# Twenty matmuls over a tile of ones in the first block of tokens, and other planning costs for early attention

## The chip, the cores and the metric

The kernel runs on one NeuronCore of a Trainium2 chip. The metric is the device time of one launch in microseconds (us). The engines are TensorE (PE in the profile, with its weight loads shown apart as PEld), VectorE (DVE), ScalarE (ACT), GpSimd (POOL), and SyncE (SP), whose queue issues nearly all the DMAs.

## What is computed

The reference is a chain of three layers on 2304 tokens of width 512. In short:

```python
scores = q @ k.T / 8 + slope[h] * -(distance)      # 4 x 8 heads, 576 tokens, width 64
scores = where(0 <= i - j < 128, scores, -1e9)     # a window of 128
x = softmax(scores) @ v                            # to 2304 x 512
h = x @ w_in                                       # 512 -> 2048
x = (h - tanh(h)) @ w_out                          # 2048 -> 512
xn, en = x / norm(x), expert_emb / norm(expert_emb)
logits = xn @ en.T / tau                           # 8 experts, the best one is taken
out = gate * (relu(x[mask] @ w1[e]) @ w2[e])       # 512 -> 1024 -> 512 for each expert
```

## The kernel before

The 2304 tokens are 18 blocks of 128, worked on two at a time (9 groups). A block's attention is cut into four quarters of two heads. A quarter is a chain over the engines: scores on TensorE (`scores`, L456, into the PSUM tile `sc`), bias and row minimum on VectorE (`soft`, L484), exponent on ScalarE (`exp`, L498), a turn of the probabilities on TensorE (`tr_pe`, L518), its copy to SBUF on ScalarE or VectorE (`tr_out`, L524, tile `ptf`), and the product with v on TensorE (`pv_f`, L535, tile `of`). This form, called early, holds for the first four blocks and runs on plain fp32 tiles; later blocks split their operands into high and low parts and turn the probabilities by DMA. A finished block is turned by four transposes (L633) into `xT`, and the two-layer part follows in steps: `g1` (L686, tile `h`, 12 matmuls of 256 columns each), tanh and a split on ScalarE and VectorE (L691 to L703), `g2` (L710, tile `acc`).

The 32 weight tiles of w_in and w_out come from HBM as 64-bit floats, each 512 KB (`rawi`, `rawo`). Each is converted by hand: a first reading on ScalarE (L325), two long integer operations on VectorE (L328, L331), and some scaling, rounding and subtracting on ScalarE, VectorE or GpSimd (L307 to L317). Nothing of a step can start before the four weight tiles that it uses are through this.

The order of the instructions on each engine is fixed when the program is built. `Plan.add` takes a task with a cost in us for each engine that could do it, a due number, and what it reads and writes; `Plan.order` places tasks one by one, each time the one that can start first by these costs (the due number decides between equals), and the engines then run their lists strictly in that order, with semaphores between them. A cost in the plan thus sets only the order and the choice of engine, never how long something takes.

At the start, `small` fills a few constants on GpSimd, among them `ones`, a 128x128 tile of bf16 ones (L237), which is first read much later, for counting tokens per expert.

Of the kernel before, what the change touches and what calls it, by code (L numbers as in the profile page):

```python
# [10 lines left out]
F32 = mybir.dt.float32  # L11
# [38 lines left out]
AHEAD = 1.5  # L50
WRATE = 1.0
WRATE2 = 1.0
PAD = 8
FA = 4
PADN = 2
# [107 lines left out]
class Builder:  # L163
# [55 lines left out]
    def consts(self, P):  # L219
# [8 lines left out]
        for h in range(H):  # L228
# [3 lines left out]
        P.add({"POOL": 0.5}, lambda e: nc.gpsimd.tensor_copy(out=self.tri, in_=at[0][:, 256:384]), -11,  # L232
              r=[("xr", 0)], w=["tri"])

    def small(self):
        nc, i = self.nc, self.i
        nc.gpsimd.memset(self.ones, 1.0)  # L237
        nc.gpsimd.memset(self.half, 0.5)
        nc.gpsimd.memset(self.cum, 0.0)
        nc.gpsimd.memset(self.oh, 0.0)  # L240
        for j in range(self.NOV):
            nc.gpsimd.memset(self.thr[:, :, j:j + 1], float(128 * j))
# [193 lines left out]
    def quarter(self, P, a, due):  # L436

        nc = self.nc
        b, qd = divmod(a, 4)
        hf, qq = divmod(qd, 2)  # L440
        s, n = b % 2, (2 * b + hf) % 2
        one = b in NOPRE
        W = 128 if one else 256
        v = {"sc": [None, None], "mx": [None, None]}
        pb = a % 2 if a < NPX else 0
# [4 lines left out]
        def scores(jj):  # L450
            sc = v["sc"][jj] = self.scores[jj][:, 0]
            j = qq + 2 * jj
            hp, p0 = hf * 4 + j, 64 * jj
            if early:
                x = slice(1, 2) if one else slice(0, 2)
                nc.tensor.matmul(sc[:, 0:W // 128, :], lhsT=self.qf[b // 2][p0:p0 + 64, b % 2, hf * 2 + qq, :],  # L456
                                 rhs=self.kf[max(b, 1)][p0:p0 + 64, x, hf * 2 + qq, :], start=True, stop=True)
                return
            q = self.qst[n]
            sl = s if one else slice(0, 2)  # L460
            for m in range(2):
                nc.tensor.matmul(sc[:, sl, :], lhsT=q[:, m, j, :], rhs=self.khl[:, sl, hp, :], start=(m == 0),  # L462
                                 stop=(m == 1))
# [116 lines left out]
        ttr += 0.13 * (2 * (b in SPLIT) + (b - 1 in SPLIT))  # L580
        for jj in range(2):
            if early:
                P.add({"PE": 0.45 if one else 0.65}, lambda e, jj=jj: scores(jj), due,
                      r=["at", ("qf", b)] + [("kf", max(b, 1), x) for x in ([1] if one else [0, 1])], w=[("sc", jj)])
            else:
                P.add({"PE": 0.11 if one else 0.22}, lambda e, jj=jj: scores(jj), due,
                      r=["at"] + ks + [("kl", x, hf) for x in kv] + q, w=[("sc", jj)])
# [7 lines left out]
        half = [("xr", 2 * hf), ("xr", 2 * hf + 1)]  # L595
        if early:
            for jj in range(2):
                P.add({"PE": 0.28 if one else 0.5}, lambda e, jj=jj: tr_pe(jj), due, r=["at", "con", ("p32", pb, jj)],
                      w=[("tp", jj)])
            for jj in range(2):  # L600
                P.add({"ACT": 0.3, "DVE": 0.29} if one else {"ACT": 0.38, "DVE": 0.42}, lambda e, jj=jj: tr_out(e, jj),
                      due, r=["at", ("tp", jj)], w=[("pt", a % 2, 1)] if jj else [("pt", a % 2), ("pt", a % 2, 1)])
            P.add({"PE": 0.85 if one else 1.65}, pv_f, due,
                  r=["at", ("pt", a % 2), ("pt", a % 2, 1)] + [("vf", x) for x in ([b] if one else [b - 1, b])], w=[("o", qq)] if qq else ["o", ("o", 0), ("o", 1)])
            if qq:
                P.add({"DVE": 0.5}, recip, due, r=["at"], w=sm)
                P.add({"DVE": 0.4}, mul, due, r=["at", "o", ("o", 0), ("o", 1)] + sm, w=half if hf else [("xr", m) for m in range(4)])
            return
# [557 lines left out]
    def build(self):  # L1166
# [7 lines left out]
        self.px = dp.tile([2 * N0, 128, DM], F32, name="px")  # L1174
        self.pa = dp.tile([2 * N0, 128, DM], F32, name="pa")
        P = Plan()
        P.add({"POOL": 0.6}, lambda e: self.small(), 0, w=["small", "cum"])
        self.consts(P)
        self.small_loads(P, -9)
        self.emb(P, -9)  # L1180
# [237 lines left out]
```

## Time and profile before

| what | us |
|---|---|
| median of three runs (843.29 to 847.38) | 847.1 |
| the profiled execution, whole | 849.56 |
| its span, from first to last instruction | 847.8 |
| TensorE busy in the span | 816.7 (96%) |
| VectorE busy | 565.5 (67%) |
| ScalarE busy | 441.6 (52%) |
| GpSimd busy | 252.1 (30%) |

The profiled execution lies 2.5 us above the median. The profile splits the span into stretches that differ in what they do: the first 66 us hold the early attention and the first steps, then the weight conversion runs on to about 143 us, and the rest is the steady run of steps, later attention, routing and experts. The shares of the whole span say little about the first two.

### The profile page before, as it was taken

What the parts mean: (1) busy time and instruction counts of PE and PEld (TensorE: products, weight loads), DVE (VectorE), ACT (ScalarE), POOL (GpSimd) and SP (SyncE); (2) the same over time, 40 slices, a digit from 0 to 9 for tenths busy, and PEclk for the clock granted to TensorE, in tenths of its full rate; (3) what the DMA queues carried; (4) which work ended last, traced back from release to release, by engine and by line L of the source; (5) the groups of instructions that cost most, each with busy time, mean ns of one, the idle gap of its engine ahead of it and who ended that gap; (6) DMA issues with size and microseconds to landing.
All of it is one profiled execution on the core that took longest, in us unless ns stands there. A gap on an engine that the chain in (4) does not pass through costs nothing.

```text
span 847.8 us, 15246 instructions
## 1 busy us (share of the span) xinstructions
PE 816.7 (96%) x5244; PEld 721.2 (85%) x5244; DVE 565.5 (67%) x1500; ACT 441.6 (52%) x997; POOL 252.1 (30%) x246
## 2 busy tenths in 40 slices
PE   6999999999999999999999999999999999999995
PEld 4677878988888899988998998989889899998994
DVE  4658999987778577777776775576366656666230
ACT  3759876665555355555554543464255545545120
POOL 1424676554424233324242240021110210111011
PEclk9999999999999999999999999999999999999998
DMA  8973325945334234433434312365266656555000
GB/s 299 334 268 121 109 94 160 270 107 130 96 82 135 40 82 106 87 87 91 99 83 102 80 41 48 125 212 162 84 198 216 216 166 189 193 163 174 20 27 30
DMA packets 109464, 112.88 MB, mean 133 GB/s; under 512 B 62901, under 2 KB 75189, under 8 KB 109248
## 3 DMA queue, kind: packets, MB, share of 16 engines
q1 hardware_dynamic: 106240, 102.35, 42.2%
q0 software_dynamic: 3136, 9.46, 3.0%
q8 instruction: 43, 0.70, 0.4%
q14 instruction: 45, 0.37, 0.1%
HBM read 87.12 MB, written 17.48 MB: 123 GB/s over the span
## 4 chain that ended last, share of the span: by engine, by line
PE 71%; DVE 11%; DMA 7%; issue 6%; ACT 2%; SPq 2%; POOL 1%; POOLq 0%; DVEq 0%; ACTq 0%
PE h L686 19%; PE acc L710 17%; PE he L1014 9%; PE y L1049 8%; PE o L546 3%; DMA pt<-ph 3%; PE sc L456 3%; PE sc L462 2%; DMA out<-yo,ix 2%; DVE wst L331 2%; PE y L1045 2%; PE misc L785 2%; PE of L535 2%; DVE rawo L328 1%; PE sc L518 1%
## 5 line engine op out<-in xcount | busy, mean ns | idle before, releaser
L686 PE MATMUL h<-xT,wi 128*128 128x256 f32 x1728 | 228.8, 287 | 0.0
L686 PEld LDWEIGHTS h<-xT,wi 128*128 128x128 f32 x1728 | 219.4, 193 | 6.4 <-issue 2.6
L710 PE MATMUL acc<-wo,gh 128*128 128x512 f32 x576 | 183.9, 400 | 0.0
L710 PE MATMUL acc<-wo,gl 128*128 128x512 f32 x288 | 112.9, 392 | 2.0 <-DVE gl L703 2.0
L710 PEld LDWEIGHTS acc<-wo,gh 128*128 128x128 f32 x576 | 99.7, 189 | 15.1 <-issue 0.7
L691 ACT ACTIVATE t<-h 128x512 f32<-128x512 f32 x72 | 43.1, 599 | 100.3 <-PE h L686 95.3
L1049 PE MATMUL y<-eo,ge 128*128 128x512 f32 x336 | 88.5, 399 | 0.0
L484 DVE CUSTOM_DVE_ANT_0 sc<-sc,bias 128x256 f32<-128x256 f32 (+1 forms) x144 | 52.7, 372 | 46.3 <-PE sc L462 29.4
L498 ACT ACTIVATE p<-sc,mx 128x256 f32<-128x256 f32 (+1 forms) x128 | 59.3, 464 | 34.1 <-DVE mx L484 26.0
L1074 POOL DMA_INDIRECT out<-yo,ix x24 | 23.4, 975 | 176.2 <-PE y L1045 61.0
L1049 PEld LDWEIGHTS y<-eo,ge 128*128 128x128 f32 x336 | 60.0, 188 | 9.7
L710 PEld LDWEIGHTS acc<-wo,gl 128*128 128x128 f32 x288 | 54.1, 188 | 15.1 <-DVE gl L703 2.9
L508 POOL TENSOR_TENSOR ph<-p,ph 128x512 f16<-128x512 f32 (+1 forms) x38 | 46.1, 1214 | 69.3 <-ACT ph L503 26.0
L703 DVE TENSOR_TENSOR gl<-t,gh 128x512 fp32r<-128x512 f32 x72 | 63.0, 876 | 4.6 <-ACT gh L699 4.4
L948 DVE TENSOR_TENSOR eo<-est,eo 128x512 fp32r<-128x512 f32 x60 | 45.0, 752 | 30.4 <-ACT eo L944 29.4
L1036 DVE SCALAR_TENSOR_TENSOR ge<-he,ge 128x256 fp32r<-128x256 f32 x104 | 29.9, 325 | 51.9 <-ACT ge L1030 51.9
L694 DVE TENSOR_TENSOR t<-h,t 128x512 f32<-128x512 f32 x72 | 49.5, 687 | 19.0 <-ACT t L691 19.0
L944 ACT CAST eo<-est 128x512 fp32r<-128x512 f32 x64 | 39.7, 620 | 40.1 <-PE y L1045 21.5
L1014 PE MATMUL he<-xT,ei 128*128 128x320 f32 x384 | 60.4, 309 | 0.0
L1014 PEld LDWEIGHTS he<-xT,ei 128*128 128x128 f32 x384 | 58.3, 188 | 2.3
L1030 ACT ACTIVATE ge<-he 128x320 fp32r<-128x320 f32 (+1 forms) x56 | 24.1, 430 | 67.5 <-PE he L1014 61.7
L1014 PE MATMUL he<-xA,ei 128*128 128x320 f32 (+1 forms) x384 | 59.0, 302 | 0.0
(181 smaller groups left out, 1425.6 us busy)
## 6 DMA issues: line engine op xcount, KB each, us to landing
est<-in_w SPq DMA_DIRECT2D x128, 256.0 KB, 2.9
rawi<-in_w_in SPq DMA_DIRECT2D x16, 512.0 KB, 6.6
rawo<-in_w_out SPq DMA_DIRECT2D x16, 512.0 KB, 7.3
stk<-in_k SPq DMA_DIRECT2D x30, 256.0 KB, 2.7
stq<-in_q SPq DMA_DIRECT2D x28, 256.0 KB, 2.8
bucket<-in_c_pad SPq DMA_DIRECT2D x8, 771.0 KB, 5.8
xe<-bucket SPq DMA_DIRECT2D x17, 257.0 KB, 3.5
vst<-in_v SPq DMA_DIRECT2D x30, 128.0 KB, 2.4
```

The source lines that it names most:

```text
L484: nc.vector.tensor_tensor_reduce(out=x, in0=x, in1=self.bias[:, h, c0:c1], scale=-0.125, scalar=mx[:, 1:2] if m else 3.0e38, op0=ALU.add, ...
L498: nc.scalar.activation(out=v["p32"][:, jj * W:(jj + 1) * W], in_=x, func=AF.Exp, scale=-1.0, bias=v["mx"][jj][:, 0:1], accum_out=self.sums ...
L508: self.eng(e).tensor_tensor(out=ph[:, 2 * W:4 * W], in0=v["p32"][:, 0:2 * W], in1=ph[:, 0:2 * W], op=ALU.subtract)
L686: nc.tensor.matmul(h3(v["h"], f2), lhsT=w[:, a, k, :], rhs=xT[c][:, :, k, :], start=(k == 0 and n == 0), stop=(k == KD - 1 and n == 2))
L691: nc.scalar.activation(out=v["t"], in_=v["h"].rearrange("p a b -> p (a b)"), func=AF.Tanh)
L694: nc.vector.tensor_tensor(out=v["t"], in0=v["h"].rearrange("p a b -> p (a b)"), in1=v["t"], op=ALU.subtract)
L703: self.eng(e).tensor_tensor(out=v["gl"], in0=v["t"], in1=v["gh"].bitcast(F32), op=ALU.subtract)
L710: nc.tensor.matmul(self.acc[g, t], lhsT=v[a][:, c0:c0 + 128], rhs=self.w["o", fs[f2]][:, c, :], start=(first and f2 == 0 and n == 0), stop ...
L944: nc.scalar.copy(out=t[:, 0, :], in_=v["x"])
L948: self.eng(eng).tensor_tensor(out=t[:, 1, :], in0=v["x"], in1=t[:, 0, :].bitcast(F32), op=ALU.subtract)
L1014: nc.tensor.matmul(h[:, 0:N], lhsT=w[:, a, c0:c0 + 128], rhs=xT()[b][:, k, 0:N], start=(k == 0 and n == 0), stop=(k == KD - 1 and n == 2))
L1049: nc.tensor.matmul(y[t], lhsT=gt(f, a)[:, (t - ts[0]) * 128:(t - ts[0] + 1) * 128], rhs=self.w["o", f0 + f][:, b, :], start=(f == 0 and n ...
```

## The change

The fill of `ones` is taken out of `small` and made a task of its own that is due first. A new function `warm` adds 20 tasks to the plan, each one matmul of `ones` with `ones` over 512 columns (bf16) into the PSUM bank `acc0`, which nothing else uses until the first step. Their results are never read. Each has a cost of 0.43 in the plan and due number 0, later than that of the attention tasks, so that the plan puts them where TensorE would have nothing else to start. The planning costs of the three TensorE tasks of early attention are set lower, to about 0.53 to 0.71 of what they were. Data and results are otherwise the same.

```diff
--- before.py
+++ after.py
@@ -50,6 +50,7 @@
 AHEAD = 1.5
 WRATE = 1.0
 WRATE2 = 1.0
+NWARM = 20
 PAD = 8
 FA = 4
 PADN = 2
@@ -232,9 +233,22 @@
         P.add({"POOL": 0.5}, lambda e: nc.gpsimd.tensor_copy(out=self.tri, in_=at[0][:, 256:384]), -11,
               r=[("xr", 0)], w=["tri"])
 
+    def warm(self, P):
+
+        nc = self.nc
+        at = {}
+
+        def mm(e):
+            if 0 not in at:
+                at[0] = self.psA.tile([128, 512], F32, tag="acc0", name="idle", bufs=1)
+            nc.tensor.matmul(at[0], lhsT=self.ones, rhs=self.ones.unsqueeze(1).to_broadcast([128, 4, 128]), start=True,
+                             stop=True)
+
+        for n in range(NWARM):
+            P.add({"PE": 0.43}, mm, 0, r=["ones"])
+
     def small(self):
         nc, i = self.nc, self.i
-        nc.gpsimd.memset(self.ones, 1.0)
         nc.gpsimd.memset(self.half, 0.5)
         nc.gpsimd.memset(self.cum, 0.0)
         nc.gpsimd.memset(self.oh, 0.0)
@@ -580,7 +594,7 @@
         ttr += 0.13 * (2 * (b in SPLIT) + (b - 1 in SPLIT))
         for jj in range(2):
             if early:
-                P.add({"PE": 0.45 if one else 0.65}, lambda e, jj=jj: scores(jj), due,
+                P.add({"PE": 0.3 if one else 0.42}, lambda e, jj=jj: scores(jj), due,
                       r=["at", ("qf", b)] + [("kf", max(b, 1), x) for x in ([1] if one else [0, 1])], w=[("sc", jj)])
             else:
                 P.add({"PE": 0.11 if one else 0.22}, lambda e, jj=jj: scores(jj), due,
@@ -595,12 +609,12 @@
         half = [("xr", 2 * hf), ("xr", 2 * hf + 1)]
         if early:
             for jj in range(2):
-                P.add({"PE": 0.28 if one else 0.5}, lambda e, jj=jj: tr_pe(jj), due, r=["at", "con", ("p32", pb, jj)],
+                P.add({"PE": 0.2 if one else 0.33}, lambda e, jj=jj: tr_pe(jj), due, r=["at", "con", ("p32", pb, jj)],
                       w=[("tp", jj)])
             for jj in range(2):
                 P.add({"ACT": 0.3, "DVE": 0.29} if one else {"ACT": 0.38, "DVE": 0.42}, lambda e, jj=jj: tr_out(e, jj),
                       due, r=["at", ("tp", jj)], w=[("pt", a % 2, 1)] if jj else [("pt", a % 2), ("pt", a % 2, 1)])
-            P.add({"PE": 0.85 if one else 1.65}, pv_f, due,
+            P.add({"PE": 0.45 if one else 0.9}, pv_f, due,
                   r=["at", ("pt", a % 2), ("pt", a % 2, 1)] + [("vf", x) for x in ([b] if one else [b - 1, b])], w=[("o", qq)] if qq else ["o", ("o", 0), ("o", 1)])
             if qq:
                 P.add({"DVE": 0.5}, recip, due, r=["at"], w=sm)
@@ -1174,7 +1188,9 @@
         self.px = dp.tile([2 * N0, 128, DM], F32, name="px")
         self.pa = dp.tile([2 * N0, 128, DM], F32, name="pa")
         P = Plan()
-        P.add({"POOL": 0.6}, lambda e: self.small(), 0, w=["small", "cum"])
+        P.add({"POOL": 0.3}, lambda e: nc.gpsimd.memset(self.ones, 1.0), -30, w=["ones"])
+        self.warm(P)
+        P.add({"POOL": 0.6}, lambda e: self.small(), 0, r=["ones"], w=["small", "cum"])
         self.consts(P)
         self.small_loads(P, -9)
         self.emb(P, -9)
```

On TensorE, the program begins with nine pairs of `LDWEIGHTS ones` and `MATMUL idle` ahead of the first two score matmuls, and four more behind these. The next piece is the start of the list of before, from the first scores (`sc_92` and `sc_93` are the two score tiles, `p` and `p32x` probabilities, `con` the identity matrix):

```order
L456 MATMUL sc_92<-kf_128,qf_126 128x128
L456 MATMUL sc_93<-kf_128,qf_126 128x128
L518 MATMUL sc_92<-con,p_160 128x128
L456 MATMUL sc_92<-kf_128,qf_126 128x128
L269 MATMUL misc<-con,ec 128x8 x4
L518 MATMUL sc_93<-con,p_160 128x128
L456 MATMUL sc_93<-kf_128,qf_126 128x128
L518 MATMUL sc_92<-con,p32x 128x128
L456 MATMUL sc_92<-kf_128,qf_126 128x128
```

The same place now, from the last of the four pairs behind the first scores:

```order
L244 LDWEIGHTS ones
L244 MATMUL idle<-ones 128x512
L532 MATMUL sc_92<-con,p_173 128x128
L470 MATMUL sc_92<-kf_131,qf_128 128x128
L283 MATMUL misc<-con,ec 128x8 x4
L532 MATMUL sc_93<-con,p_173 128x128
L470 MATMUL sc_93<-kf_131,qf_128 128x128
L244 LDWEIGHTS ones
L244 MATMUL idle<-ones 128x512
```

The first turn of probabilities (L518, now L532) stood right behind the first scores and now has 13 of the 20 added matmuls ahead of it, four of them between the two; the other seven follow, in ones and twos, up to the end of the first block. Behind them no added matmul stands.

On VectorE, the list of before at its first weight tile, in the last quarter of the first block (`rawi` and `wst` belong to the weight conversion; `sm`, `sc`, `mx`, `xr` and `ptf` to attention):

```order
L309 TENSOR_SCALAR wst<-rawi_203 128x512
L328 SCALAR_TENSOR_TENSOR rawi_203<-rawi_203 128x512
L553 TENSOR_SCALAR sm<-sm 128x4
L554 RECIPROCAL sm<-sm 128x4
L484 ISA sc_92,mx_260<-sc_92,bias 128x256
L484 ISA mx_260 128x1
L484 ISA sc_93,mx_267<-sc_93,bias 128x256
L484 ISA mx_267 128x1
L331 SCALAR_TENSOR_TENSOR wst<-wst,rawi_203 128x512
L572 TENSOR_TENSOR xr<-of,sm 128x256
L313 CAST wi_283<-wst 128x512
L328 SCALAR_TENSOR_TENSOR rawi_220<-rawi_220 128x512
```

The same place now:

```order
L323 TENSOR_SCALAR wst<-rawi_223 128x512
L538 COPY ptf<-sc_92 128x128
L567 TENSOR_SCALAR sm<-sm 128x4
L568 RECIPROCAL sm<-sm 128x4
L498 ISA sc_92,mx_279<-sc_92,bias 128x256
L498 ISA mx_279 128x1
L498 ISA sc_93,mx_284<-sc_93,bias 128x256
L498 ISA mx_284 128x1
L586 TENSOR_TENSOR xr<-of,sm 128x256
L342 SCALAR_TENSOR_TENSOR rawi_223<-rawi_223 128x512
L538 COPY ptf<-sc_92 128x256
L345 SCALAR_TENSOR_TENSOR wst<-wst,rawi_223 128x512
```

The two long operations of the first weight tile (L328 and L331, now L342 and L345) have moved behind the softmax of the next quarter and the output of the block before; attention is taken a little earlier against the weights. Further down the two lists hold the same tasks in about the same mixture.

## Rows read from the trace of the kernel before

**Rows 1.** The page: busy time of the engines, and the granted clock in 40 slices
```profile
PE 816.7 (96%) x5244; PEld 721.2 (85%) x5244; DVE 565.5 (67%) x1500; ACT 441.6 (52%) x997; POOL 252.1 (30%) x246
...
PEclk9999999999999999999999999999999999999998
```

**Rows 2.** The chain of waits from 5 to 66 us: share by line
```profile
by line: PE sc L456 34.7%; PE of L535 21.5%; PE sc L518 14.6%; PE h L686 14.1%; DMA ec<-in_emb 5.0%; PE misc L633 3.1%; ACT wst L307 1.7%; ACT ptf L524 1.7%; ACT p L498 1.5%; issue 1.5%; ACT p32x L498 1.5%; ACT rawi L325 0.9%; PE misc L269 
```

**Rows 3.** The chain of waits from 66 to 143 us: share by line
```profile
by line: DVE wst L331 23.9%; DVE rawo L328 16.2%; DVE rawi L328 11.1%; DVE gl L703 10.9%; DVE t L694 6.3%; issue 6.0%; DVE sc L484 4.6%; DVE xT L646 3.2%; DVE sm L553 3.1%; DVE wst L309 2.3%; DVE wo L317 2.2%; ACT ptf L524 1.5%; DVE sc L469
```

**Rows 4.** Busy time of each engine by stretch (header names the columns)
```profile
core 0: us, PE busy (x) PEld busy (x) DVE busy (x) ACT busy (x) POOL busy (x), PEclk, DMA share, GB/s
8.00:20.00 12.00, 12.00 (x39) 8.08 (x38) 5.70 (x27) 5.25 (x18) 1.27 (x1) 1.00 1.01 351
20.00:40.00 20.00, 19.00 (x65) 12.93 (x64) 12.25 (x33) 14.66 (x40) 7.73 (x7) 1.00 1.03 357
40.00:66.00 26.00, 26.00 (x96) 19.82 (x94) 16.11 (x40) 15.46 (x40) 6.37 (x7) 1.00 0.73 265
66.00:80.00 14.00, 13.23 (x83) 9.75 (x83) 11.91 (x29) 12.46 (x33) 4.68 (x3) 1.00 0.18 63
80.00:143.00 63.00, 57.54 (x374) 50.49 (x374) 62.10 (x81) 48.84 (x96) 46.99 (x32) 1.00 0.36 114
143.00:848.00 705.00, 687.47 (x4588) 619.15 (x4588) 453.72 (x1278) 342.87 (x767) 182.97 (x173) 0.99 0.43 120
```

**Rows 5.** TensorE in order of time, 54 to 76 us: start, us, what
```profile
54.99 1.80 PE L535 MATMUL of<-vf,ptf 128*128 128x64 f32 x8
...
57.88 2.93 PE L686 MATMUL h<-xT,wi 128*128 128x256 f32 x12
...
61.16 1.22 PE L456 MATMUL sc<-kf,qf 64*128 64x256 f32 x2
62.31 2.93 PE L686 MATMUL h<-xT,wi 128*128 128x256 f32 x12
...
67.51 1.71 PE L686 MATMUL h<-xT,wi 128*128 128x256 f32 x12
69.06 1.00 PE L535 MATMUL of<-vf,ptf 128*128 128x64 f32 x8
...
71.17 0.70 PE L456 MATMUL sc<-kf,qf 64*128 64x256 f32 x2
...
73.01 0.73 PE L710 MATMUL acc<-wo,gh 128*128 128x512 f32 x2
```

**Rows 6.** Who VectorE waited for, 5 to 66 us: total, times, longest
```profile
DVE sc L484 <- ACT ptf L524: 11.2, 11, 2.4
```

**Rows 7.** All engines in order of time, 0 to 9 us
```profile
0.86 0.20 POOL L237 MEMSET ones<- 128x128 bf16 x1 [0.29 <-POOLq L1410]
...
5.46 0.80 PE L456 MATMUL sc<-kf,qf 64*128 64x128 f32 x4 [5.46 <-DMA kf<-in_k]
...
7.30 0.47 PE L518 MATMUL sc<-con,p 128*128 128x128 f32 x1 [1.04 <-ACT p L498]
```

**Rows 8.** Line 325, the first reading of a weight tile, up to 66 us
```profile
L325 ACT ACTIVATE rawi<-rawi x11: 667/678/717, 16.5 to 65.8; 128x512 int32<-128x512 uint32 x11
L325 ACT ACTIVATE rawo<-rawo x6: 645/677/687, 28.7 to 64.7; 128x512 int32<-128x512 uint32 x6
...
  DMA rawi<-in_w_in: 0.4, 1
```

**Rows 9.** DMA issues up to 36 us: count, KB each, us to landing
```profile
rawi<-in_w_in SPq DMA_DIRECT2D x10, 512.0 KB, 8.6
rawo<-in_w_out SPq DMA_DIRECT2D x6, 512.0 KB, 8.5
```

**Rows 10.** TensorE alone: one thin stretch, and after the last matmul
```profile
120.70:124.00 3.30, 1.54 (x7) 1.00 0.90 318
840.00:842.00 2.00, 0.00 (x0) 0.71 0.36 135
```

## Prediction

> **What bounds the kernel now.** I read the page first. TensorE is busy 96% of the span, and the granted clock reads full in all slices but the last [rows 1], so the page alone says that only less TensorE work can help. I then asked which instructions the chain of waits runs over, stretch by stretch, because the share is a mean over stretches with different limits. Up to 66 us the chain is TensorE's: scores 34.7%, product with v 21.5%, turns 14.6%, first steps 14.1% [rows 2]. From 66 to 143 us it is VectorE's, above all the two long operations of the weight conversion [rows 3]; VectorE is then busy 62.10 of the 63 us from 80 on [rows 4]. Behind 143 us TensorE is busy 687.47 of 705 us, and nothing of that stretch is touched.
>
> Next I compared one form with itself at different times, which no share shows. Twelve `h` matmuls took 2.93 us at 62.31 and 1.71 us at 67.51; a pair of scores 1.22 us at 61.16 and 0.70 at 71.17; eight products with v 1.80 at 54.99 and 1.00 at 69.06 [rows 5]. The ratios are 0.58, 0.57 and 0.56, in three forms, all within some 5 us. [...] Before the rise TensorE was busy nearly all the time, but with short fp32 pieces; it rose at the end of the stretch with the `h` matmuls of 62.31. A TensorE that looks busy with such pieces had thus stayed at the low level for 60 us.
>
> **What the change does, part by part.**
>
> *The clock.* Nine matmuls of 512 columns run in a row from about 1.1 us, when `ones` is filled (0.86 + 0.20, [rows 7]), with no operand from HBM; four more follow the first scores. They are dense like the `h` matmuls that came just before the rise. I take it that the clock rises at about 8 us instead of 66. At the low level 12 matmuls of 256 columns take 2.93 us, 0.24 each, so one of 512 columns is at most about 0.49 us there, and at the full level at most 0.73 / 2 = 0.37 (two of `acc`, [rows 5]); both are estimates from a group with its last end in it.
>
> *TensorE's own saving.* From 8 to 66 us it was busy 12.00 + 19.00 + 26.00 = 57.0 us [rows 4]. At 0.575 of that it needs 32.8 us: 24.2 us less. That is the gain if nothing else holds it up.
>
> *What is late next.* In the same 58 us VectorE did 5.70 + 12.25 + 16.11 = 34.1 us of work and ScalarE 5.25 + 14.66 + 15.46 = 35.4 us [rows 4]. This work has to be done as well before the state of 66 us is reached. Much of VectorE's idle time was a wait in attention: 11.2 us ahead of `soft`, put down to ScalarE's copy, which itself lies behind TensorE's turn [rows 6]. How densely VectorE and ScalarE work when TensorE is at full level and the rest is the same mixture of attention and conversion, is shown by the stretch from 66 to 80 us: 11.91 and 12.46 of 14 us, 85% and 89% [rows 4]. At these densities 34.1 us of VectorE take 40.0 us, and 35.4 us of ScalarE 39.7 us. Begun at 8 us, the state of 66 us is reached at 48: 18 us earlier. TensorE's 32.8 us fit in that. This is the term that I take, not the 24.2, since VectorE bounds the next 77 us as well and nothing in them gets faster.
>
> *What comes off.* The first nine added matmuls need up to 9 x 0.49 = 4.4 us, from 1.1 to 5.5 us, and TensorE waited for the first k until 5.46 [rows 7], so they are hidden there, or cost 0.1 us. The next four (up to 2.0 us at the low level) stand ahead of the first turn, which waited 1.04 us for ScalarE [rows 7]: they delay it by up to 0.9 us. The last seven cost at most 7 x 0.37 = 2.6 us at the full level, and lie in the slack that TensorE then has (40 us for 33 us of work). The filling of `ones` moves ahead of nothing that waits. The first weights can't come earlier: the DMA engines' share is 1.01 and 1.03 from 8 to 40 us [rows 4], and ScalarE's first reading of a weight, at 16.5 us, waited for its DMA [rows 8]. By 66 us 17 weights had been read [rows 8]; 16 were issued by 36 us and landed 8.5 us later [rows 9], by about 45, so for a state reached at 48 us they come just in time. I take 1 us for that.
>
> *The planner's costs and the moved tasks.* They shift the conversion of the first tiles on VectorE a little behind attention. VectorE's total is unchanged, and it is the total that I have counted; I set this at nothing, between -2 us (attention, on which TensorE waits, comes earlier) and +2 us (weights come later in the stretch that VectorE bounds).
>
> *The sum.* 18.0 - 0.9 - 1 = 16 us. The profiled execution took 849.56 us, so 833.5; it lies 2.5 us above the median, so the median should be 831 us.
>
> [...]
>
> **The rivals.**
> - *The clock doesn't rise early.* The added matmuls come in a burst, then scores stand between, and attention goes on in short pieces, with which TensorE stayed low for 60 us. The burst is longer than one `h` group (2.93 us); but one group alone, at 57.88 us, was followed by scores that still took 1.22 us, at 61.16 [rows 5], so the rise isn't certain. If the clock rises only with the `h` matmuls again, the added work stands in TensorE's chain: 0.1 + 0.9 + 7 x 0.49 = 4.4 us, and the median is 851.5: slower. Each us that the clock rises later costs some 16 / 58 = 0.28 us of the gain, and 12 us at the full level pay for the last seven matmuls (3.4 us): it decides from a rise later than about 54 us.
> - *It rises and falls back.* Early attention alone may not hold it. For this: nothing in the trace shows a long stretch of attention alone at the full level. Against it: at 120.7 to 124.0 us TensorE was busy 1.54 of 3.30 us and stayed up, and the level fell only after the last matmul, at 840 to 842 us [rows 10]; from 69.06 to 73.01 only attention ran, at the full level [rows 5]. If it is low for half of the 40 us, half the gain is left: 8 us, 839. [...]
> - *The transfers hold it.* If the conversion before 40 us can't move at all, since its weights arrive at the DMA engines' full rate, only the 26 us from 40 to 66 shrink: VectorE's 16.11 us at 85% take 18.9 us, a gain of 7.1 us, 840. Against it: VectorE itself waited mostly for attention there [rows 6].
> - *VectorE gets no gaps at all.* From 8 to 143 us it was busy 34.1 + 11.91 + 62.10 = 108.1 of 135 us [rows 4]; with no idle time left, 26.9 us are gained: 820. For this it would need to be denser than from 66 to 80 us, while ScalarE has its share in every quarter.
>
> **How the numbers follow.** The forecast (824 to 836) has 0.55, the full gain 0.06, the falling back 0.06, the transfers 0.07, no early rise 0.20, and a rise somewhere in between, which leaves 1 to 4 us, 0.06. About half a per cent, 4.2 us, can be told from no change. The first four are faster: 0.74, less 0.02 for their edges. Of no early rise, at 851.5 with the limit at 851.3, I give 0.14 to slower and 0.06 to the same, to which the rise in between adds its 0.06 and the edges 0.02. The range has to reach over no early rise, since it alone holds 0.20: 821 to 852. The forecast's own range is 824 to 836.
>
> **What would show it.** In the changed profile: the `idle` matmuls from about 1.1 us; pairs of scores of 256 columns at 0.70 us, not 1.22, from the second block on; the first `h` group at 1.7 us and some 12 to 18 us earlier than at 50; the chain of waits going over from TensorE to VectorE or ScalarE before 30 us; VectorE's dense stretch ending at about 127 us, not 143; and the stretch behind it as long as before. Pairs of scores at 1.22 us up to 50 us would show the prediction wrong; so would early pairs at 0.70 with the dense stretch still ending at 143.

## The result and the profile after

The changed kernel took 851.1 us (median of 20 runs, 846.38 to 855.65) against 846.2 us of the kernel before in the same sessions (20 runs): a ratio of 1.0067, 95% interval 1.0054 to 1.0080. It is 0.7% slower. The forecast was 831 us and faster: wrong in its sign, though the range 821 to 852 holds the time. That 851.1 lies beside the 851.5 of the rival without an early rise is chance, since the clock did rise early here, at 6.63 us. The profiled execution of the changed kernel took 849.39 us, 0.17 us less than that of before; the two medians lie 4.9 us apart. At 849.56 us the traced execution of before took longer than any of its 20 runs (843.29 to 848.67). So differences between these two traces show where time moves, and the sizes come from the medians and ratios below.

The page after, as in [rows 1]: busy time, and the granted clock in 40 slices of 21.2 us.

```profile
PE 816.5 (96%) x5264; PEld 716.8 (85%) x5264; DVE 570.0 (67%) x1500; ACT 440.5 (52%) x993; POOL 257.5 (30%) x250
...
PEclk9579899999999999999999999999999999999998
```

The clock now has a dent in the second and third slices, and a smaller one in the fifth. TensorE in order of time (start, us, what, and in brackets the idle time before it) answers to [rows 5] and [rows 7]:

```profile
1.12 4.02 PE L244 MATMUL idle<-ones 128*128 128x512 bf16 x9 [1.12 <-POOL half L252]
5.16 0.80 PE L470 MATMUL sc<-kf,qf 64*128 64x128 f32 x4
5.89 1.38 PE L244 MATMUL idle<-ones 128*128 128x512 bf16 x4
7.11 0.27 PE L532 MATMUL sc<-con,p 128*128 128x128 f32 x1
...
19.91 0.70 PE L470 MATMUL sc<-kf,qf 64*128 64x256 f32 x4
20.54 1.28 PE L549 MATMUL of<-vf,ptf 128*128 128x64 f32 x8
23.23 0.44 PE L532 MATMUL sc<-con,p32x 128*128 128x128 f32 x2 [1.41 <-ACT p32x L512]
23.60 1.15 PE L470 MATMUL sc<-kf,qf 64*128 64x256 f32 x2
...
25.30 1.22 PE L470 MATMUL sc<-kf,qf 64*128 64x256 f32 x2
...
46.49 2.93 PE L700 MATMUL h<-xT,wi 128*128 128x256 f32 x12
...
50.92 1.72 PE L700 MATMUL h<-xT,wi 128*128 128x256 f32 x12
```

The burst does what was forecast of it: the record has the clock at full from 6.63 us, the first scores begin at 5.16 us instead of 5.46, and the first turn at 7.11 instead of 7.30. At 19.91 us four score matmuls take 0.70 us. But at 23.60 us two of them take 1.15 us and then 1.22, as before, and this lasts until an `h` group ends at about 51 us: the first group at 46.49 us takes 2.93 us, the next 1.72. The record has the lower level, 0.50 of the full clock, from 23.70 to 51.01 us. So full speed was won from 6.6 to 23.7 us and from 51 to 66 us, and not between.

The stretches after (us, busy time and count of PE, PEld, DVE, ACT, POOL, then granted clock, share of the DMA engines, GB/s):

```profile
8.00:24.00 16.00, 12.82 (x70) 8.14 (x69) 11.30 (x39) 10.30 (x34) 2.16 (x2) 0.99 1.05 367
24.00:51.00 27.00, 27.00 (x87) 17.54 (x86) 15.26 (x40) 14.79 (x40) 9.32 (x8) 0.50 0.97 340
51.00:66.00 15.00, 14.61 (x102) 11.87 (x103) 11.92 (x32) 12.44 (x35) 3.84 (x3) 1.00 0.60 196
66.00:143.00 77.00, 69.40 (x415) 59.55 (x415) 73.04 (x96) 58.08 (x115) 50.33 (x34) 0.96 0.39 129
143.00:200.00 57.00, 54.76 (x417) 49.11 (x416) 48.94 (x153) 35.52 (x93) 36.68 (x36) 1.00 0.66 164
```

The same stretches of the kernel before:

```profile
8.00:24.00 16.00, 15.67 (x50) 10.35 (x50) 8.04 (x34) 8.44 (x27) 2.60 (x2) 1.00 1.00 349
24.00:51.00 27.00, 26.33 (x91) 18.21 (x90) 17.24 (x46) 17.83 (x49) 9.83 (x10) 1.00 0.92 322
51.00:66.00 15.00, 15.00 (x60) 12.27 (x59) 8.78 (x23) 9.09 (x24) 2.94 (x3) 1.00 0.71 264
66.00:143.00 77.00, 70.78 (x456) 60.25 (x456) 74.01 (x109) 61.30 (x128) 51.68 (x35) 1.00 0.33 105
143.00:200.00 57.00, 55.28 (x419) 50.33 (x420) 46.30 (x148) 36.34 (x92) 29.37 (x31) 1.00 0.71 188
```

VectorE is 3.3 us ahead at 24 us, 1.3 us ahead at 51 and 4.4 us ahead at 66. From 24 to 51 us, with both kernels at the low level (pairs of scores at 1.22 us in both), the changed order does *less* of VectorE's work (15.26 us against 17.24). The two lists of VectorE do not go on in about the same mixture, as the section on the change has it: counted in the traces, the second long operation (L331, now L345) of the tenth tile is VectorE's 125th instruction before and its 147th after. TensorE's idle time from 66 to 200 us is 7.60 + 2.24 = 9.8 us, against 6.22 + 1.72 = 7.9 before. The waits of TensorE after, from 66 to 200 us (total us, times, longest):

```profile
PE h L700 <- DVE t L708: 4.2, 3, 3.3
PE sc L476 <- POOL qst L384: 1.3, 1, 1.3
PE o L560 <- DMA pt<-ph: 1.3, 2, 0.8
PE h L700 <- POOL wi L331: 1.2, 3, 0.8
```

The last subtraction of the weight conversion, before on VectorE and after on GpSimd, in order of time:

```profile
140.64 1.77 DVE L317 TENSOR_TENSOR wo<-wst,wo 128x512 fp32r<-128x512 f32 x1
```
```profile
144.79 1.28 POOL L331 TENSOR_TENSOR wo<-wst,wo 128x512 fp32r<-128x512 f32 x1 [1.28 <-ACT wo L327]
```

The conversion was to end at about 127 us; it ends at 146.1 us, 3.7 us later than before. Counted by the ends of groups of 12 `h` matmuls, the changed kernel leads by 6.4 to 7.5 us at the 7th to the 10th group (86 to 102 us) and by 4.7 us at the 25th (149.6 against 154.3), and is 0.5 us behind at the 34th (191.5 against 191.0). The lead is earned before 90 us, and given back between 95 and 191 us, a stretch in which the change has moved the order and added nothing.

### The profile page after: what moved, and what is told of

It reads as the page before. It is cut to its first block, busy times and chain, and to the rows that moved or that the text cites. A ratio compares the mean times of both kernels' runs of the same rounds, so it can differ in the third digit from the quotient of the medians.

```text
span 847.6 us, 15293 instructions
## 1 busy us (share of the span) xinstructions
PE 816.5 (96%) x5264; PEld 716.8 (85%) x5264; DVE 570.0 (67%) x1500; ACT 440.5 (52%) x993; POOL 257.5 (30%) x250
## 4 chain that ended last, share of the span: by engine, by line
PE 69%; DMA 9%; DVE 8%; issue 6%; ACT 3%; SPq 2%; POOL 2%; POOLq 0%; DVEq 0%; ACTq 0%
PE h L700 18%; PE acc L724 15%; PE he L1028 10%; PE y L1063 8%; DMA pt<-ph 5%; PE o L560 3%; DMA out<-yo,ix 2%; PE y L1059 2%; PE sc L470 2%; PE sc L476 2%; DVE wst L345 2%; PE of L549 2%; PE misc L799 1%; PE sc L532 1%; DVE gl L717 1%
## 5 line engine op out<-in xcount | busy, mean ns | idle before, releaser
L700 PEld LDWEIGHTS h<-xT,wi 128*128 128x128 f32 x1728 | 220.2, 194 | 13.2 <-DVE t L708 5.0
L1088 POOL DMA_INDIRECT out<-yo,ix x24 | 23.4, 975 | 177.4 <-PE y L1059 62.0
L717 DVE TENSOR_TENSOR gl<-t,gh 128x512 fp32r<-128x512 f32 x72 | 65.5, 909 | 7.4 <-ACT gh L713 7.0
L724 PEld LDWEIGHTS acc<-wo,gl 128*128 128x128 f32 x288 | 54.1, 188 | 13.7 <-DVE gl L717 1.6
L522 POOL TENSOR_TENSOR ph<-p,ph 128x512 f16<-128x512 f32 (+1 forms) x36 | 44.2, 1227 | 65.4 <-ACT ph L517 31.6
```

What stands on the lines that cost most here:

```text
L522: self.eng(e).tensor_tensor(out=ph[:, 2 * W:4 * W], in0=v["p32"][:, 0:2 * W], in1=ph[:, 0:2 * W], op=ALU.subtract)
L700: nc.tensor.matmul(h3(v["h"], f2), lhsT=w[:, a, k, :], rhs=xT[c][:, :, k, :], start=(k == 0 and n == 0), stop=(k == KD - 1 and n == 2))
L717: self.eng(e).tensor_tensor(out=v["gl"], in0=v["t"], in1=v["gh"].bitcast(F32), op=ALU.subtract)
L724: nc.tensor.matmul(self.acc[g, t], lhsT=v[a][:, c0:c0 + 128], rhs=self.w["o", fs[f2]][:, c, :], start=(first and f2 == 0 and n == 0), stop ...
```

## The experiments

Two things were mixed: the burst (clock) and the order (lower costs, and 20 x 0.43 us of planned time). The theory from these rows: the burst works and does not last, and the order costs. Its rival: the order is harmless, and the short early rise by itself upsets what follows. Ratios are to runs of the kernel before on the same chip, with 95% intervals.

**The order alone.** In the changed kernel the 20 tasks emit nothing:

```diff
-            P.add({"PE": 0.43}, mm, 0, r=["ones"])
+            P.add({"PE": 0.43}, lambda e: None, 0, r=["ones"])
```

> The changed kernel's order of tasks to the letter, but none of the twenty matmuls is emitted, so the clock should rise only with the first h groups, at about 50 to 65 us. Theory A (the new order costs time: it puts attention ahead of the weight conversion on VectorE, and an early clock has to pay for that): 852 to 856 us, slower than the changed kernel's 851. Theory B (the order is harmless, the added matmuls are what costs): 845 to 848, as the kernel before. The third reading of a tile by the second long operation of the conversion should come some 3 to 8 us later than before under A.

This took 852.9 us (median of 6), ratio 1.0095 (1.0065 to 1.0125). The clock rises at 55.7 us. The third of the second long operations ends at 43.5 us, 7.8 us later than before (35.7), as expected under A. The conversion's last subtraction, on GpSimd, begins at 149.84 us and ends at 151.1, 8.7 us later than before. The order costs about 6 us, where the forecast's outer bound was 2.

**The burst alone.** The order of before, nothing moved; the matmuls over ones are emitted inside the existing tasks, 9 ahead of the first scores, then 4, 2, 3 and 2 behind the scores of the first four quarters:

```diff
+IDLE0 = 9
+IDLE_SC = {0: 4, 1: 2, 2: 3, 3: 2}
+IDLE_TR = {}
...
+    def idle(self, n):
+        for _ in range(n):
...
+            self.nc.tensor.matmul(self.xi["idle"], lhsT=self.ones, rhs=self.ones.unsqueeze(1).to_broadcast([128, 4, 128]),
+                                  start=True, stop=True)
...
+                self.idle(IDLE0 if a + jj == 0 else 0)
...
+                self.idle(IDLE_SC.get(a, 0) * jj)
...
+            self.idle(IDLE_TR.get(a, 0) * jj)
```

> The kernel before with its order of all other tasks unchanged on every engine; the twenty matmuls over ones are put into it at nearly the places that they have in the changed kernel (nine ahead of the first scores, eleven in the first block). Theory A: the clock rises at about 7 us and falls back at 20 to 27 us, when attention alone runs, and VectorE's conversion is not pushed back: 839 to 843 us, faster than before by 0.4 to 0.8%. Theory B: the matmuls cost and the short high level returns nothing: 848 to 852.

846.9 us, ratio 0.9996 (0.9975 to 1.0017). The clock is full from 4.1 to 11.0 us, then low until 55.3 (0.50 granted from 24 to 51 us). TensorE ahead of the fall at 10.96 us (stretch and columns as above):

```profile
8.00:10.96 2.96, 2.85 (x17) 1.85 (x17) 1.88 (x9) 1.26 (x6) 0.00 (x0) 1.00 0.94 347
```

So a burst that does not hold returns nothing, and harms nothing; the rival falls. The medians of this kernel and the changed one lie 4.2 us apart, the ratios 0.7% (6 us). That is put down to the order; but the full level lasted 7 us in this trace and 17 in the changed one, so the pair does not differ in the order alone.

**Holding the clock, first try.** The same `idle` calls in quarters 4 to 11 (second and third block) too: 2 behind the scores, 2 behind the turns. Once in the changed order with its own 20 (a3_hold), once in the order of before (a4_burst_hold):

```diff
+IDLE_SC = {4: 2, 5: 2, 6: 2, 7: 2, 8: 2, 9: 2, 10: 2, 11: 2}
+IDLE_TR = {4: 2, 5: 2, 6: 2, 7: 2, 8: 2, 9: 2, 10: 2, 11: 2}
```

> The changed kernel's order, with two matmuls over ones behind the scores and two behind the turns of each of the eight quarters of blocks 1 and 2 (32 more, some 7 us of TensorE at the full level). Theory C (the gain is missing because the clock falls back at 24 us): it stays up from 7 us on, and the time is 832 to 838. Theory A (the order of the conversion on VectorE is what costs): the clock stays up, but the end of the conversion hardly moves, and the time is 843 to 848.

> The kernel before with its order unchanged, with both the burst of the first block and the 32 matmuls of blocks 1 and 2. Theories A and C together: the clock stays up from 7 us on, VectorE isn't kept waiting by TensorE and the conversion isn't pushed back, 828 to 836 us. If VectorE and ScalarE are bound by the transfers of the weights instead: 838 to 843.

847.2 us, 1.0000 (0.9975 to 1.0026), with the clock full from 4.3 to 11.1 us and from 24.8 to 82.8; and 844.0 us, 0.9970 (0.9946 to 0.9993), full from 5.4 to 19.0 us and from 42.9 to 118.0. The profiled execution of the second, 847.1 us, is one of its slower ones, with a mean clock of 0.980; the seven with 0.988 to 0.990 took 839.6 to 844.0 us. The fill holds the clock partly, and where it does some time comes back; the order of before is again the better one, by 3 us.

**Holding it with more.** 4 behind scores and 4 behind turns in quarters 1 to 11; in the order of before (b1_hold4), and in the changed one on top of its 20 (b2_hold4_order):

```diff
+IDLE_SC = {1: 4, 2: 4, 3: 4, 4: 4, 5: 4, 6: 4, 7: 4, 8: 4, 9: 4, 10: 4, 11: 4, 0: 4}
+IDLE_TR = {1: 4, 2: 4, 3: 4, 4: 4, 5: 4, 6: 4, 7: 4, 8: 4, 9: 4, 10: 4, 11: 4}
```

> The order of the kernel before, the burst ahead of the first scores, and four matmuls over ones behind the scores and four behind the turns of each quarter from the first block to the third (88 in the quarters, twice as many per quarter as in a4_burst_hold, where the clock still fell from 19 to 43 us). Theory C (what is missing is a clock that stays up): up from about 5 us to the end of the stretch, 834 to 840 us. Theory D (with the clock up, VectorE and ScalarE in their fixed order take over, and the added matmuls, some 20 us of TensorE, stand in attention's chain): 841 to 845, no better than a4_burst_hold's 844.

> The same added matmuls in the changed kernel's order. Theory A (the order itself costs some 5 us through the conversion, whatever the clock does): 3 to 6 us slower than b1_hold4. If the order suits a fast clock and only cost because the clock fell: equal to b1_hold4 or faster.

846.2 us, 0.9997 (0.9980 to 1.0014), and 850.5 us, 1.0043 (1.0023 to 1.0063). Nothing was gained. In the second the clock held from 6.6 to 85 us, and the chain of waits from 8 to 66 us, by line, says why:

```profile
by line: PE idle L254 34.0%; PE sc L478 21.4%; PE of L559 12.5%; PE sc L541 11.1%; PE h L710 8.6%; PE acc L734 2.7%; PE misc L657 2.5%; ACT rawi L346 2.2%; issue 1.1%; ACT wi L334 1.1%; ACT p32x L521 0.8%; ACT p L521 0.8%; ACT ptf L548 0.8%
```

There the filling itself became TensorE's bound: what the clock gave, the fill took. For the first kernel this is not shown. In its profiled execution the same burst raised the clock only at 19.8 us, and that execution took 851.2 us, 5 us more than the median.

**Is it only that the conversion comes late?** The changed kernel with due numbers of the conversion lowered: by 5 without the 20 matmuls (b3_conv_first), by 2 with them (c4_due2):

```diff
+        due -= 5
```

> As a1_order (the changed kernel's costs and planned tasks, none of the matmuls emitted; 852.85 us), but the due numbers of the conversion tasks are 5 earlier, those of the loads unchanged. On VectorE the 13th tile's second long operation stands at row 92 instead of 156, before it was 146. Theory A (the costs push the conversion back on VectorE, and that is what takes the 6 us): 843 to 848 us, back to the kernel before or better. If the loss comes in another way (attention, transfers, POOL): 850 to 858.

> The changed kernel with its twenty matmuls and its costs, but the due numbers of the conversion tasks 2 earlier, so that VectorE's list has the conversion a little earlier than before's (the 16th tile's second long operation at row 152; changed 167, before 166; the 10th at 117, 133 and 120). Theory A: the conversion ends at or before 142 us, and the time is 842 to 847, better than the changed kernel's 851. If attention is starved by it, as in b3_conv_first: over 853.

871.2 us, 1.0279 (1.0250 to 1.0307), and 865.7 us, 1.0224 (1.0186 to 1.0262): much slower. TensorE's waits in the first, from 24 to 143 us:

```profile
PE sc L533 <- ACT p L513: 7.9, 3, 5.5
PE sc L477 <- ACT p L513: 7.6, 1, 7.6
PE sc L533 <- ACT p32x L513: 6.3, 3, 3.1
```

Now attention starves behind the conversion. "The conversion is late" is no sufficient cause: it seems to matter how the two interleave, and before's mixture is the best of those that were run.

**What VectorE's time is worth.** The kernel before, with the first long operation of the conversion issued twice:

```diff
-            out=v["L"], in0=v["H"], scalar=-2 ** 31, in1=v["L"], op0=ALU.bitwise_and, op1=ALU.bitwise_or),
+            out=v["L"], in0=v["H"], scalar=-2 ** 31, in1=v["L"], op0=ALU.bitwise_and, op1=ALU.bitwise_or) for _ in range(2)],
```

> The kernel before, with the first long operation of the conversion (line 328) issued twice for each of the 32 tiles; the second one repeats what the first did, and the result is the same. It adds 32 x 0.6 to 1.0 us, 20 to 30 us, to VectorE, about a third of it ahead of 66 us. If VectorE's work bounds the stretch from 66 to 143 us one to one, the time grows by 15 to 25 us (862 to 872), less what its waits before 66 us take up. If it is the transfers or TensorE that bound it: under 855.

861.9 us, 1.0180 (1.0157 to 1.0203). 589.9 - 565.5 = 24.4 us more of VectorE cost 14.8 us. Of the added work 48.73 - 37.75 = 11.0 us lie ahead of 66 us, in time that was idle before: the first `h` group ends at 53.0 us in both. The other 13.4 us put off the end of the conversion by 13.2 us (155.6 against 142.4). So VectorE does bound the stretch behind 66 us, about one for one, as the forecast had it. The clock fell three times in this trace (at 69.9, 87.0 and 131.3 us); what share that has is not known.

**Less work on TensorE instead of a faster clock.** In the look-back quarters half of the products with v and half of the turns are left out; in the order of before (c1_half) and in the changed one without its 20 (c2_half_order):

```diff
-            for x in range(W // 128):
+            for x in range(W // 128 if a < 5 else 1):
...
-                for kb in range(KB):
+                for kb in range(1):
```

> The order of the kernel before, no matmuls over ones. In the twelve quarters of the early blocks that look back, half of the products with v (the earlier block's share of the sum) and from the second such quarter on half of the turns are left out, so the output isn't the reference's; scores, softmax, copies and the conversion are all still done. It takes some 1.0 + 0.5 us of TensorE at the low level out of each quarter, 17 us in all, as a higher clock would, but without any filling matmul. The prediction's step (VectorE and ScalarE close up to 85 to 89% as soon as TensorE is quicker): 832 to 837 us. Theory E (the lists of VectorE and ScalarE are fixed, with the conversion in between as it suits a slow TensorE; they close up only a little): 840 to 844.

> The same left out, in the changed kernel's order of tasks, without its twenty matmuls. If the changed order is the right one for a quick TensorE: equal to c1_half or faster. Theory A (the order costs whatever the clock does, since the conversion ends later): 4 to 7 us slower than c1_half, 844 to 850.

847.2 us, 1.0004 (0.9988 to 1.0020), and 846.2 us, 0.9996 (0.9980 to 1.0013). Inconclusive for its purpose: with less to do TensorE fell back to the low level again and again (in the first from 52.9 to 56.4, 66.6 to 70 and 87 to 90.5 us), so the two effects are mixed. The pair shows one thing: with this lighter attention the changed order is not slower, so its cost isn't fixed.

**Between the two fills.** 9 ahead and 4 behind the first scores, then per quarter 3 behind the scores and 1 (quarters 1 to 3) or 2 (4 to 11) behind the turns, 9 + 4 + 33 + 19 = 65 matmuls. In the order of before (c3_hold_mid), in the changed order without its own 20 (d1_mid_order), and in the order of before without the first 13 (d2_no_burst, `IDLE0 = 0`, no entry 0):

```diff
+IDLE0 = 9
+IDLE_SC = {1: 3, 2: 3, 3: 3, 4: 3, 5: 3, 6: 3, 7: 3, 8: 3, 9: 3, 10: 3, 11: 3, 0: 4}
+IDLE_TR = {1: 1, 2: 1, 3: 1, 4: 2, 5: 2, 6: 2, 7: 2, 8: 2, 9: 2, 10: 2, 11: 2}
```

> The order of the kernel before, the burst, and in the quarters up to the third block three matmuls over ones behind the scores and one or two behind the turns (between a4_burst_hold's two and two and b1_hold4's four and four). If the clock stays up by this, and the fill is cheap enough: 839 to 843 us, better than a4_burst_hold's 844. If the fill takes what the clock gives, as in b1_hold4: 845 to 847.

> The matmuls over ones of c3_hold_mid (the same number at the same quarters, clock up from 4 us on there, 839.9 us), in the changed kernel's order of tasks, whose own twenty are not emitted. If the changed order is the better one once the clock stays up (c2_half_order was no slower than c1_half): 833 to 840 us. If the changed order costs by itself (a1_order against the kernel before, 6 us; b2_hold4_order against b1_hold4, 4 us): 843 to 847.

> c3_hold_mid without the nine matmuls ahead of the first scores and the four behind them; the fill of the later quarters is the same. If the burst is what raises the clock and the fill only holds it: the clock rises late or at varying times, 844 to 848 us. If the fill raises it by itself within the first block: 839 to 842, as c3_hold_mid.

The first took **839.9 us, ratio 0.9922 (0.9899 to 0.9944)**: faster than both kernels. Its clock is full from 4.0 to 109.9 us. TensorE in order of time, the stretches, and the chain of waits from 8 to 66 us by line:

```profile
24.96 0.59 PE L242 MATMUL idle<-ones 128*128 128x512 bf16 x2
25.49 0.70 PE L467 MATMUL sc<-kf,qf 64*128 64x256 f32 x4
26.12 0.82 PE L242 MATMUL idle<-ones 128*128 128x512 bf16 x3
26.78 1.10 PE L548 MATMUL of<-vf,ptf 128*128 128x64 f32 x8
```
```profile
8.00:24.00 16.00, 14.97 (x82) 9.09 (x82) 10.51 (x39) 9.94 (x32) 3.94 (x3) 1.00 1.04 366
24.00:51.00 27.00, 26.37 (x154) 17.13 (x154) 22.44 (x56) 22.57 (x61) 11.70 (x10) 1.00 1.06 378
51.00:66.00 15.00, 14.41 (x95) 11.05 (x93) 13.23 (x32) 14.09 (x35) 4.76 (x3) 1.00 0.54 201
66.00:143.00 77.00, 71.72 (x469) 63.12 (x468) 74.30 (x122) 57.34 (x120) 52.23 (x37) 0.98 0.46 139
```
```profile
by line: PE sc L467 21.3%; PE idle L242 16.2%; PE sc L530 9.6%; PE of L548 8.1%; PE h L699 8.1%; ACT ptf L537 3.8%; ACT p32x L510 3.7%; DVE sc L496 3.1%; DVE rawi L338 3.0%; DVE sm L566 2.4%; DVE rawo L338 2.0%; ACT rawi L335 2.0%; ACT p L5
```

With the clock held, VectorE works 22.44 of 27 us (83%) and then 13.23 of 15 (88%), and the conversion ends at 129.2 us (its last subtraction begins at 127.38). The fill is still 16.2% of the chain of waits, some 9 us, so no run shows what a held clock is worth without its fill. The same fill in the changed order took 849.7 us, 1.0029 (1.0000 to 1.0057), and eleven of its twelve runs spread from 842.7 to 853.5. Its profiled one, 842.74 us, is one of the fastest, with the clock full from 4.6 to 79.7 us; the slower of these runs (847.9 us and more), all but one, have lower mean clocks (0.981 to 0.988, against 0.989 to 0.992 of the four fastest), which points to a clock held for less long. The profiled one is 2.8 us behind the 839.97 of the other order. With the clock full in both, VectorE had done 10.84 + 20.60 + 12.33 = 43.8 us of work from 8 to 66 us, against 46.2. So in these two traces the order costs time with a quick TensorE too. Without the burst the order of before took 849.7 us, 1.0027 (1.0005 to 1.0049): its clock rises at 33.3 us. The burst is needed; it is just not enough.

**Which half of the order's change.** The lower planning costs alone (e1_costs), and the 20 tasks planned but emitting nothing, with the old costs and `ones` filled first (e2_tasks); no added matmul in either:

```diff
-                P.add({"PE": 0.45 if one else 0.65}, lambda e, jj=jj: scores(jj), due,
+                P.add({"PE": 0.3 if one else 0.42}, lambda e, jj=jj: scores(jj), due,
...
-            P.add({"PE": 0.85 if one else 1.65}, pv_f, due,
+            P.add({"PE": 0.45 if one else 0.9}, pv_f, due,
```

> The kernel before with the three lower planning costs alone; no added matmuls, no added tasks, ones filled where it was. TensorE stays at the low level until some 55 to 66 us as in the kernel before. If the lower costs of early attention are what costs the 6 us of the changed order, it takes about 853 (ratio 1.006 to 1.010) and the last subtraction of the weight conversion ends at 146 us or later, with GpSimd busy some 36 us from 143 to 200 us. If the 8.6 us of planned TensorE time are the cause, it is no slower than before: 845 to 849.

> The old planning costs, but the twenty tasks stand in the plan with 0.43 each and emit nothing, and ones is filled first. If the planned TensorE time of these tasks shifts the order so that 6 us are lost, about 853 (ratio 1.006 to 1.010), conversion ending later than 146 us. If the lower costs are the cause, 845 to 849 and a conversion that ends at about 142 us. If each has a share, both kernels lie at 848 to 851.

858.2 us, 1.0149 (1.0123 to 1.0175), and 849.5 us, 1.0036 (1.0021 to 1.0051). The lower costs are the cause: alone they cost some 11 us, more than was expected and more than with the tasks beside them (6). The planned time of the tasks alone costs 2 us, and beside the lower costs takes back part of their harm. The tenth tile's second long operation is VectorE's 148th instruction with the costs alone and its 122nd with the tasks alone, against 147th and 125th in the two kernels. With the tasks alone the conversion ends at 137.6 us, 4.8 us earlier than before, and the kernel is slower all the same, so that end does not settle the time. The stretches of the kernel with the costs alone:

```profile
24.00:51.00 27.00, 27.00 (x87) 17.68 (x86) 15.84 (x42) 15.87 (x44) 7.07 (x6) 1.00 0.79 264
51.00:66.00 15.00, 14.70 (x69) 10.62 (x68) 7.54 (x25) 8.53 (x24) 5.03 (x5) 1.00 0.96 357
66.00:143.00 77.00, 67.28 (x429) 58.41 (x428) 73.21 (x102) 60.98 (x125) 46.43 (x32) 0.98 0.35 114
143.00:200.00 57.00, 51.41 (x366) 45.10 (x366) 50.79 (x149) 34.99 (x89) 36.16 (x33) 0.99 0.71 175
```

From 24 to 66 us VectorE does 15.84 + 7.54 = 23.4 us of work, against 17.24 + 8.78 = 26.0 before: it idles while attention, ahead in its list, waits for a TensorE at the low level (pairs of scores at 1.22 us up to 52.92). From 24 to 66 us it waits 3.5 us for products with v, before 1.0, and 9.9 us for ScalarE's copies of turned probabilities, before 8.6. The fifth of the long second operations of the conversion ends at 59.7 us, before at 42.0. The conversion ends at 151.5 us, and TensorE idles 9.72 + 5.59 = 15.3 us from 66 to 200 us, 7.4 more than before, where the two profiled spans differ by 856.4 - 847.8 = 8.6. That count also goes with the order's cost in the other pairs: 9.8 us in the changed kernel against 7.4 in the burst alone, where the spans differ by 847.6 - 845.1 = 2.5; 9.9 us in the changed order with the middle fill against 6.8 in the old one, spans 841.1 and 838.2.

## Why the prediction was wrong, step by step

*The bound before* was read rightly. TensorE at the low level did hold the first 66 us (pairs of scores took 1.22 us from 17.54 us on to 61.16, and 0.70 at 71.17), and VectorE the stretch behind: with the clock held, time was gained (c3_hold_mid), with more VectorE work behind 66 us it was lost (b4_twice).

*The clock's early rise* came, at 6.6 us for "about 8". The nine matmuls were hidden, and the four behind them cost the first turn nothing, where 0.9 us was taken off.

*The failed step is that the clock, once up, stays up.* The sum took the full level from 8 us on as given, and the rival of falling back got 0.06. The argument against it was [rows 10], a stretch busy 1.54 of 3.30 us at the full level, and 4 us of attention alone in [rows 5]. In the changed kernel two stretches, each just ahead of a fall, read:

```profile
82.00:85.00 3.00, 1.52 (x10) 1.32 (x11) 3.00 (x5) 0.90 (x2) 0.90 (x1) 1.00 0.86 264
20.90:23.70 2.80, 1.39 (x10) 0.98 (x9) 2.47 (x7) 2.80 (x9) 1.86 (x2) 1.00 1.03 392
```

Ahead of the falls at 23.70 and 85.14 us TensorE was busy 1.39 of 2.80 and 1.52 of 3.00 us, about half of the time as in [rows 10], and the level fell all the same. One stretch that held said too little. Nor did a busy TensorE hold the level by itself: in the burst alone it was busy 2.85 of 2.96 us ahead of the fall at 10.96 us. And once down it stayed down for 27 us in which TensorE was busy all of the time, with the kind of pieces that had gone with the low level for 66 us before. The prediction had seen that such pieces had not raised the clock in 60 us, and didn't ask whether they hold it. The fall at 98.79 us came at the end of 3.30 us without a matmul; those at 23.70 us, behind a wait of 1.41 us, and in the burst alone at 10.96 us came without such a pause. What made the level fall at 23.70 us, where the prediction lost its gain, stays open; the rival of falling back should have had most of the weight for what it said first, that nothing in the trace showed a long stretch of attention alone at the full level.

*The rivals' size of the falling back* (half the gain left, 839) failed too. The burst alone left nothing (846.9). Its clock was up for 7 us only, but the changed kernel's was for 17, and of VectorE's lead of 3.3 us at 24 us 1.3 are left at 51. In the changed order the 20 matmuls return 852.9 - 851.1 = 1.8 us, the ratios 1.0095 and 1.0067, whose intervals overlap: little, if anything.

*The planner's costs and the moved tasks, "at nothing, between -2 and +2"*, is the second failed step, and it makes the sign. The order costs 6 us by itself, and with the burst the medians lie 4.2 us apart. The reasoning was that VectorE's total is unchanged. But a total bounds an engine only while it is busy: the changed order puts attention ahead of the conversion, and with TensorE slow VectorE idles in its place. The experiment with the costs alone shows this directly, at some 11 us. That costs set for the full clock were wrong for a kernel that is mostly below it there fits these runs, but it is argued and not the whole: also with the clock held this order was the slower one, by 2.8 us in the profiles, and with the lighter attention it was not. Why is not settled, nor why the tasks' planned time takes back part of the costs' harm.

*What is late next, VectorE and ScalarE at 85% and 89%*: right in kind, a little too dense. With the clock held, VectorE's 34.1 us of work from 8 us on are done at 51 + (34.06 - 32.95) / 0.88 = 52.3 us, where 48 was forecast, since from 8 to 24 us it came to 10.51 of 16 us only. The DMA engines' share is 1.04 there, but VectorE waits only 0.7 us for a weight and ScalarE 1.7, and TensorE with the fill is busy 14.97 of the 16 us; which of the two held that part is not shown. The lead of 13.7 us is still there at the 25th `h` group (141.0 us against 154.3) and mostly at the 67th (298.6 against 310.5); the whole profiled execution is 9.6 us shorter, and the median 7.2 us, since the profile of before lies 2.5 us above its median. Of the 2.3 us lost behind the 67th group, TensorE's idle time from there to the end of the span accounts for 2 (539.65 - 522.81 = 16.8 us, against 537.34 - 522.53 = 14.8 before); what it waits for there was not followed.

*The sum, mended*: a gain of 7.2 us where the clock holds by a fill, instead of 16, gives 840; falling back takes nearly all of that (847); the order then adds 4 to 6 (851 to 853).

## What to carry to other kernels

Ask of a faster clock two questions, what raises it and what holds it, and look for a stretch of the same kind of work at the full level before counting on the second; here four or five dense matmuls in each quarter, behind a burst, held it from 4.0 to 109.9 us (ratio 0.9922), while eight gained nothing (0.9997). A planner's costs move work even where no total changes, here by some 11 us, so change speed and costs one at a time. A lead in an early stage can be worth less than its length: 13 us at 150 us were 9.6 us at the end of the same execution.

## What the runs showed of the hardware that was not expected

- In the changed kernel the clock fell twice more, long behind the start: the record has the lower level from 85.14 to 88.55 us and from 98.79 to 102.21 us, each time behind a thin place of TensorE (1.52 of 3.00 us busy, and 3.30 us idle), and it stayed low while dense `h` matmuls ran. 24 of them took 4.62 us each time (after, first two lines), where 24 in a row took 3.12 us at the full level (before, third line):

```profile
84.10 4.62 PE L700 MATMUL h<-xT,wi 128*128 128x256 f32 x24 [0.53 <-DVE t L708]
...
98.81 4.62 PE L700 MATMUL h<-xT,wi 128*128 128x256 f32 x24 [3.30 <-DVE t L708]
```
```profile
92.04 3.12 PE L686 MATMUL h<-xT,wi 128*128 128x256 f32 x24
```

These falls go with the order. The order alone has them too (at 89.8 and 103.4 us), and every other trace in the changed order (the changed kernel, a3, b2, c2, d1) has one or two that begin between 79 and 99 us; of those in the order of before with its work unchanged (the kernel before, a2, a4, b1, c3, d2) none falls between 67 and 109 us. The two falls cost TensorE 2 x 1.5 = 3 us by these lines; how much of the order's 4 to 6 us that is, is not shown.

- The same program did not always get the same clock. In 3 of the 20 runs of the changed kernel the record shows a mean granted clock of 0.992, as it does where no early rise is recorded (0.993 in the order alone), and these took 854.7 to 855.7 us, three of the four slowest; the others read 0.964 to 0.977. The mean can be higher where the clock was low for longer: in the kernel before the record reads 1.00 from 8 to 66 us, while pairs of scores take 1.22 us there, so a mean near 1 is not to be read as a clock that was up. The burst of b1_hold4 shows the same in a trace: its nine matmuls start at 1.12 us as in c3_hold_mid, and the level rose at 19.8 us there (four matmuls over ones took 1.82 us at 18.01, and 0.86 at 21.12) and at 4.0 us here.
